# Own products of four token tiles in one stretch, another order of the first steps, short warming products and shifted due times

## The chip, the cores and the metric

The kernel runs on one core of one Trainium2 chip. The metric is device microseconds of one execution: the median of several runs. A trace is taken of one execution. TensorE (PE) multiplies matrices, VectorE (DVE), ScalarE (ACT) and GpSimd (POOL) work element by element, and SyncE (SP) issues the DMA transfers.

## What is computed

An attention-like scan over 4 batches, 8 heads, 768 tokens, head width 32 and state width 16, in chunks of 32 tokens, is followed by two feed-forward layers of width 256 to 2048 to 256 over all 3072 tokens. All is fp32.

```python
# attention, per chunk of 32 tokens
CB = np.einsum('bhin,bhjn->bhij', Cc, Bc)
M = CB * L                                   # L: decays within the chunk, causal
y_intra = np.einsum('bhij,bhjd->bhid', M, xc)
y_inter = np.einsum('bhin,bhnd->bhid', Cc, state) * decay_to_i[:, :, :, None]
y[:, :, sl] = y_intra + y_inter
state = decay_full[:, :, None, None] * state + np.sum(Bx, axis=2)
...
h = x @ w_in                                 # layer 1
x = np.maximum(0.01 * h, h) @ w_out
...
h = x @ w_in2                                # layer 2
out = (h * np.cos(h)) @ w_out2
```

## The kernel before

**Tiling.** The 3072 tokens are six blocks of 512; a block is 128 tokens of each batch, so four token tiles of 128 tokens (one for each batch). Attention runs in chunks of 64 tokens. Every fp32 product of the feed-forward layers is made of three fp32r products: the operands are split into a high part (hi) and a remainder (lo), and hi·hi, lo·hi and hi·lo are added in PSUM. ScalarE makes most of the hi parts, GpSimd and VectorE make lo.

**Stages.** `attention(b)` (L802) makes the layer's input x1h/x1l for block b. For block 0 each tile goes by itself: `cb` (L661, products of C and B), `products` (L709: y within the chunk and the new state, the "own" products), `carried` (L722, from the state before), in pairs of tiles. For blocks 1 to 5 one call does all four tiles' C·B products, two calls do the own products of two tiles each (L858 to L861, with a pause of `APART` = 4.2 planned between them, in which other products go), and one does the carried products of all four. Tile 0 and 1 of a pair hand states (st) on, which VectorE and ScalarE make from PE's results. `layer(b)` (L879) does layer 1 of blocks 0 to 3 in 16 steps f over the 2048 hidden columns: six products into h (L906 to L908), the leaky relu, the split, and six into y (L931 to L933). In blocks 0 and 1 the first `HALVES` = 3 steps are done for the first half of the tokens, then for the second half (256 columns each, L886 to L888). Blocks 4 and 5 of layer 1 and all of layer 2 go in pairs of blocks by a scheme with fewer products (`pair`, L1013; its output products are L1114 to L1116). Weights come in fp32 and are split on the chip (`weights`, L443).

**What sets the order.** Each operation is entered in a list (`Order.add`) with a due time, or with none; `set_due` (L113) then computes one backwards from what needs it, less a slack. `Order.run` (L121) plays through the program with a planned cost for each operation and lets every engine take the ready operation with the earliest due time; operations marked "turn" (the layers' products) go in a fixed order. The instructions are then issued in that order, so each engine's queue is fixed when the kernel is built. Buffers are rings of a few slots (`SLOTS`).

**Warming products.** `warm` (L315) issues products of two-byte zeros that nobody reads, so that PE has work in the head: the first `WARM_FIRST` = 11 are due before everything else, the rest fill PE's pauses in the plan until the first layer product is placed; what is left of the `WARM` = 150 is dropped. 24 of them, of 512 columns, are in the program.

Of the kernel before, what the change touches and what calls it, by code (L numbers as in the profile page):

```python
# [3 lines left out]

# [20 lines left out]
NB, H, S, D, N = 4, 8, 768, 32, 16  # L25
# [3 lines left out]
NBLK = S // T  # L29
NT = NB * NBLK  # L30
KF = DFF // 128
WARM = 150
WARM_N = 512
WARM_FIRST = 11
STEP = 2.85
PAIR_STEP = 10.6
OUT_BY = 2.0
# [6 lines left out]
ALONE = 2  # L44
SOON = 14.0
AHEAD = 8.0
WITHIN = 1.5
HEAD = 14.0
HALVES = 3
HALVED = 2  # L50
HALF_STEP = 1.55
STAGGER = 1.0
# [4 lines left out]
APART = 4.2  # L57
# [30 lines left out]
class Order:  # L88
# [24 lines left out]
    def set_due(self, after):  # L113
        for o in reversed(self.ops):
            by = o["by"] if o["by"] is not None else o["due"] if o["due"] is not None else float("inf")
            took = min(o["engines"].values()) + self.GAP + o["lag"]
            o["by"] = min([by] + [self.ops[m]["by"] - took for m in after[o["n"]]])
            if o["due"] is None:
                o["due"] = o["by"] - o["slack"]

    def run(self):  # L121
        ops, writer, readers, users = self.ops, {}, {}, {}
# [122 lines left out]
def scan_moe_kernel(ctx: ExitStack, tc, tokp, headp, abc, w_in, w_out, w_in2, w_out2, out):  # L245
# [4 lines left out]
    V, A, G, PE, SP = E["V"], E["A"], E["G"], E["P"], E["S"]  # L250
# [18 lines left out]
    od = Order(SLOTS, ("tok", "head", "abc"))  # L269
    tiles = {"A": ps.tile([128, 2, 512], F32, tag="att", bufs=1, name="att")}  # L270
# [44 lines left out]
    def warm(e, i):  # L315
        if i == 0:
            make("spread", "y", [128, H, Q], F32)
            make("warm", "h", [128, 512], F32)
        PE.matmul(tiles["warm"][:, 0:WARM_N], lhsT=tiles["zero"][:, 0:128], rhs=tiles["zero"][:, 0:WARM_N], start=True, stop=True)

    if WARM:
        od.add(-200, {"V": 0.2}, warm_zero, writes=["zero"], make=[("zero", "hi")])
        for i in range(WARM):
            od.add(-200 if i < WARM_FIRST else 1e6, {"P": WARM_N / 1200}, lambda e, i=i: warm(e, i), reads=["zero"] + (["warm/x"] if i else []),
                   writes=["warm/x"] + ([] if i else ["spread"]), make=[] if i else [("spread", "y"), ("warm", "h")], lag=-Order.GAP, spare=True)


# [474 lines left out]
    def attention(b, due, by, slack):  # L802
# [8 lines left out]
        if plain:  # L811
            od.add(due, {"N": 0.0}, fresh, reads=[f"x1h{b - 1}/fresh"] if b else [],
                   writes=[f"x1{p}{b}/fresh" for p in "hl"], make=[(f"x1{p}{b}", f"x1{p}") for p in "hl"])
# [8 lines left out]
        def on_pe(cost, group, steps, reads, writes, make=()):  # L822

            def go(e):
                for f in steps:
                    f()
            od.add(None, {"P": cost}, go, reads=reads, writes=writes, make=make, slack=min(x.slack for x in group))

        if first:
            for x in tt:  # L830
                attention_loads(x.t, x.slack)
            for i in (0, 2):
                pair = tt[i:i + 2]
                for x in pair:
                    x.prepare()
                    new = [(n, "g") for n in att_names(x.t)] if x.j == 1 else []
                    on_pe(0.6, [x], [x.cb], [*(f"x1l{b}/{j}" for j in range(i)), x.head + "/b", x.head + "/c", *(keys([x], "/y") if i else [])],
                          [*keys([x], "/cb"), *(n + "/y" for n, _ in new)], new)
                for x in pair:
                    x.decays()  # L840
                for x in pair:
                    on_pe(0.66, [x], [x.products], [x.tok + "/b", x.tok + "/x", x.ab, *keys(pair, "/cb")], [*keys([x], "/s"), *keys(pair, "/y")])
                for x in pair:
                    x.carries()
                for x in pair:
                    on_pe(0.3, [x], [x.carried], [x.head + "/c", *x.st[x.s0:2], *keys(pair, "/y")], keys(pair, "/y"))
                pair[0].outputs()
        else:
            k = Block(b, tt)
            for x in tt:  # L850
                attention_loads(x.t, x.slack)
            for x in tt:
                x.prepare()
            on_pe(1.25, tt, [k.fresh, *(lambda x=x: x.all_cb(x.j == 0) for x in tt)], [*(x.head + n for x in tt for n in ("/b", "/c")), f"run{b - 1 if b < PLAIN else b - 2}"],
                  k.keys("/cb", "/y", "/s"), [(n, "g") for n in k.names[1:]])
            for x in tt:
                x.decays()
            for i in (0, 2):  # L858
                on_pe(1.35, tt[i:i + 2], [x.products for x in tt[i:i + 2]],
                      [n for x in tt[i:i + 2] for n in (x.tok + "/b", x.tok + "/x", x.ab)] + ([f"apart{b}.0"] if i else []), k.keys("/cb", "/y", "/s"))  # L860
                od.add(None, {"D": APART}, lambda e: None, reads=k.keys("/s"), writes=[f"apart{b}.{i}"], slack=tt[0].slack)  # L861
            for s in range(1 if b == NBLK - 1 else 2):
                od.add(None, {"V": 0.36 + 0.1 * s}, lambda e, s=s: k.mask(s), reads=["own", *k.keys("/s")], writes=[tt[s].tok + "/x"], slack=tt[0].slack)
            for x in tt:
                x.carries()
            on_pe(1.2, tt, [x.all_carried for x in tt], [f"apart{b}.2", *(n for x in tt for n in (x.head + "/c", *x.st[0:2]))], k.keys("/y"))
            for s in range(2) if not plain else ():
                od.add(None, {"A": 0.6 + 0.1 * s}, lambda e, s=s: k.x_full(e, s),
                       reads=[*([n + "/y" for n in k.names[1:]] if s else ["A/y"]), *(f"x1f{b}/{c}" for c in range(2))], writes=[f"x1f{b}/{c}" for c in range(2)], slack=tt[0].slack)
            for p, e in (("h", "A"), ("l", "V")) if plain else ():  # L870
                for s in range(2):
                    od.add(None, {e: 0.6 + 0.1 * s}, lambda e, s=s, f=(k.x_hi if p == "h" else k.x_lo): f(s),
                           reads=[f"x1h{b}/fresh", f"x1l{b}/fresh", *([n + "/y" for n in k.names[1:]] if s else ["A/y"]), *([f"x1h{b}/{j}" for j in range(NB)] if p == "l" else [])],
                           writes=[f"x1{p}{b}/{j}" for j in range(NB)], slack=tt[0].slack)
# [4 lines left out]
    def layer(b, T0):  # L879

        n = NB * T
        d = STEP
# [1 line left out]
        ys = [f"y0.{b}.{c}" for c in range(2)]  # L884
        half = slice(0, n // 2), slice(n // 2, n)
        if b < HALVED:  # L886
            steps = [(f, q, T0 + (HALVES * i + f) * HALF_STEP) for i, q in enumerate(half) for f in range(HALVES)]
            T0 += 2 * HALVES * HALF_STEP - HALVES * d  # L888
        else:
            steps = []  # L890
        steps += [(f, slice(0, n), T0 + f * d) for f in range(len(steps) // 2, KF)]

        for f, q, at in steps:
            m = q.stop - q.start
# [286 lines left out]

    at = [HEAD]
    for b in range(PLAIN):
        at.append(at[b] + KF * STEP + (2 * HALVES * HALF_STEP - HALVES * STEP if b == 0 else 0))
    T0 = [at[PLAIN] - EARLY + 8 * PAIR_STEP * i for i in range(NBLK // 2 + 1)]

    weights(0, 0.0)
# [79 lines left out]
```

## Time and profile before

| | |
|---|---|
| median of 3 runs | 560.75 us (560.06 to 560.77) |
| profiled execution | 560.45 us |
| its span | 558.7 us, mean granted clock 0.99 |
| PE busy | 549.6 us, 98% of the span |
| VectorE, ScalarE, GpSimd busy | 436.5, 405.8, 251.1 us |
| HBM traffic | 46.50 MB read, 14.78 MB written, 110 GB/s over the span |

The span is cut by PE: the other engines have room on average. What PE waits for, and at which clock it runs, is in the table of waits and the table of windows. "Issue" as a releaser means that no semaphore explains the idle time. Granted clock 1.00 is 2.4 GHz, 0.50 is 1.2 GHz. A product of fp32 operands is shown in the trace as two passes, so 8 of them are x16. Times of an instruction reach from its start to its end; products overlap in PE, and the distance from start to start is what one costs in a dense row.

### The profile page before, as it was taken

How to read it: one execution, taken by the hardware profiler on the slowest of the kernel's cores; microseconds unless marked ns; L12 is line 12 of the kernel's file. 1: busy time of each engine (PE TensorE's matmuls, PEld its weight loads, DVE VectorE, ACT ScalarE, POOL GpSimd, SP SyncE). 2: the span in 40 equal slices, each digit the busy share in tenths (PEclk: the TensorE clock that was granted, in tenths of full speed). 3: DMA queues.
4: the chain of work that ended last, by engine and by line, in shares of the span. 5: the costliest groups of instructions: out<-in, count | busy, mean ns of one | idle time of the engine just before them, and what ended most of it. 6: DMA issues, size and time to landing. Idle time of an engine off the chain costs nothing.

```text
span 558.7 us, 11394 instructions
## 1 busy us (share of the span) xinstructions
PE 549.6 (98%) x4228; PEld 448.3 (80%) x4230; DVE 436.5 (78%) x833; ACT 405.8 (73%) x728; POOL 251.1 (45%) x255
## 2 busy tenths in 40 slices
PE   8899999999999999999999999999999999999996
PEld 3688897887888888888888788888888888888885
DVE  6789969998999556665655787877887878878776
ACT  4899868567668866666544788876887868867764
POOL 4502131031210644998100359955469853554540
PEclk9699999999999999999999999999999999999999
DMA  8993382757859730254344100000200000200002
GB/s 264 293 301 124 115 282 94 237 199 243 302 190 320 249 120 35 66 163 146 120 156 142 38 1 1 1 1 2 75 0 2 0 2 0 76 1 2 0 1 76
DMA packets 34632, 62.01 MB, mean 111 GB/s; under 512 B 3121, under 2 KB 12337, under 8 KB 34577
## 3 DMA queue, kind: packets, MB, share of 16 engines
q1 hardware_dynamic: 34432, 61.16, 32.9%
q8 instruction: 33, 0.54, 0.4%
q14 instruction: 23, 0.18, 0.1%
q10 hardware_dynamic: 144, 0.13, 0.1%
HBM read 46.50 MB, written 14.78 MB: 110 GB/s over the span
## 4 chain that ended last, share of the span: by engine, by line
PE 95%; DVE 2%; issue 1%; DMA 1%; ACT 0%; SPq 0%; DVEq 0%; ACTq 0%
PE h L906 6%; PE y L931 6%; PE h L907 5%; PE h L908 5%; PE y L932 5%; PE y L933 5%; PE y L1116 5%; PE h L1047 5%; PE att L1116 5%; PE y L1114 5%; PE y L1115 5%; PE att L1115 5%; PE att L1114 5%; PE h L1049 5%; PE h L1048 5%; PE g L1049 4%
## 5 line engine op out<-in xcount | busy, mean ns | idle before, releaser
L82 POOL TENSOR_TENSOR lo<-u,hi 128x512 fp32r<-128x512 f32 (+1 forms) x114 | 143.6, 1280 | 164.9 <-ACT hi L82 123.2
L82 ACT ACTIVATE hi<-u 128x512 fp32r<-128x512 f32 (+1 forms) x147 | 88.2, 614 | 10.3 <-DVE u L82 9.3
L82 ACT ACTIVATE k<-k,half_pi 128x512 f32<-128x512 f32 x96 | 68.2, 722 | 8.6 <-DVE k L82 8.4
L82 ACT ACTIVATE u<-h 128x512 f32<-128x512 f32 (+1 forms) x70 | 39.8, 570 | 40.9 <-PE h L908 40.7
L906 PE MATMUL h<-x1h,wi 128*128 128x512 f32 (+1 forms) x140 | 54.5, 389 | 0.0
L931 PE MATMUL y<-hi,wo 128*128 128x512 f32 (+1 forms) x140 | 53.4, 381 | 0.0
L907 PE MATMUL h<-x1l,wi 128*128 128x512 f32 (+1 forms) x140 | 53.0, 378 | 0.0
L908 PE MATMUL h<-x1h,wi 128*128 128x512 f32 (+1 forms) x140 | 52.9, 378 | 0.0
L932 PE MATMUL y<-hi,wo 128*128 128x512 f32 (+1 forms) x140 | 52.4, 374 | 0.0
L933 PE MATMUL y<-lo,wo 128*128 128x512 f32 (+1 forms) x140 | 52.3, 373 | 0.0
L82 DVE TENSOR_TENSOR g<-tmp,g 128x512 f32<-128x512 f32 x64 | 44.3, 692 | 8.2 <-PE g L1049 6.3
L1116 PE MATMUL y<-lo,wo 128*128 128x512 f32 x128 | 50.0, 391 | 0.3 <-DVE lo L82 0.3
L1116 PE MATMUL att<-lo,wo 128*128 128x512 f32 x128 | 49.8, 389 | 0.0
L1115 PE MATMUL y<-hi,wo 128*128 128x512 f32 x128 | 49.8, 389 | 0.0
L1115 PE MATMUL att<-hi,wo 128*128 128x512 f32 x128 | 49.8, 389 | 0.0
L1114 PE MATMUL y<-hi,wo 128*128 128x512 f32 x128 | 49.8, 389 | 0.0
L1114 PE MATMUL att<-hi,wo 128*128 128x512 f32 x128 | 49.8, 389 | 0.0
L82 ACT ACTIVATE k<-h 128x512 int32<-128x512 f32 x48 | 28.7, 597 | 23.4 <-PE h L1049 23.0
L82 DVE TENSOR_TENSOR u<-g,k 128x512 f32<-128x512 f32 x48 | 33.0, 687 | 11.5 <-ACT k L82 11.0
L82 DVE SCALAR_TENSOR_TENSOR k<-k,h 128x512 f32<-128x512 int32 x48 | 32.7, 682 | 10.0 <-ACT k L82 10.0
L82 DVE TENSOR_TENSOR lo<-u,hi 128x512 fp32r<-128x512 f32 (+1 forms) x52 | 35.5, 685 | 5.0 <-ACT hi L82 4.6
L82 ACT ACTIVATE k<-g 128x512 int32<-128x512 f32 x48 | 28.5, 594 | 12.3 <-DVE g L82 12.1
(269 smaller groups left out, 1467.1 us busy)
## 6 DMA issues: line engine op xcount, KB each, us to landing
head<-headp SPq DMA_DIRECT2D x24, 256.0 KB, 4.4
tok<-tokp SPq DMA_DIRECT2D x24, 256.0 KB, 4.9
abc<-a_clip SPq DMA_DIRECT2D x40, 128.0 KB, 3.7
raw<-w_out SPq DMA_DIRECT2D x8, 512.0 KB, 4.9
wi<-kept_wi SPq DMA_DIRECT2D x8, 512.0 KB, 4.8
wo<-kept_wo SPq DMA_DIRECT2D x8, 512.0 KB, 3.9
raw<-w_in SPq DMA_DIRECT2D x7, 512.0 KB, 4.8
ws<-kept_ws SPq DMA_DIRECT2D x8, 384.0 KB, 3.5
```

The lines of the kernel that those rows point to most:

```text
L82: self.seen.append(call(*args, **kwargs))
L906: PE.matmul(o, lhsT=wh, rhs=xh, start=(c == 0), stop=False)
L907: PE.matmul(o, lhsT=wh, rhs=xl, start=False, stop=False)
L908: PE.matmul(o, lhsT=wl, rhs=xh, start=False, stop=(c == 1))
L931: PE.matmul(o, lhsT=wh, rhs=gh, start=(f == q.start == 0), stop=False, **skip)
L932: PE.matmul(o, lhsT=wl, rhs=gh, start=False, stop=False, **skip)
L933: PE.matmul(o, lhsT=wh, rhs=gl, start=False, stop=(f == KF - 1), **skip)
L1047: PE.matmul(o, lhsT=wh, rhs=xh, start=start, stop=False, skip_group_check=True)
L1049: PE.matmul(o, lhsT=wl, rhs=xh, start=False, stop=True, skip_group_check=True)
L1114: PE.matmul(o, lhsT=wh, rhs=gh, start=begin, stop=False, skip_group_check=True)
L1115: PE.matmul(o, lhsT=wl, rhs=gh, start=False, stop=False, skip_group_check=True)
L1116: PE.matmul(o, lhsT=wh, rhs=gl, start=False, stop=end, skip_group_check=True)
```

## The change

Five things are changed. The own products of the four tiles of a block (blocks 1 to 5) are one call, hence one stretch in PE's queue, and the planned pause of 4.2 stands behind it. The warming products are of two lengths: the first 58 have 96 columns, the later ones 512. The first steps of block 0 go in the order 0, 2, 3 for each half, then 1 for all tokens. After the due times are computed, a table of seeds shifts some of them: each seed moves every operation, with a chance of 15%, by up to 3 either way; nine seeds for those due before 62, five for those due from 440 on. Constants become tuples for this.

```diff
@@ -1,5 +1,6 @@
 import bisect
 import heapq
+import random
 from contextlib import ExitStack
 
 import numpy as np
@@ -29,9 +30,9 @@
 NBLK = S // T
 NT = NB * NBLK
 KF = DFF // 128
-WARM = 150
-WARM_N = 512
-WARM_FIRST = 11
+WARM = 197
+WARM_N = 96, 512
+WARM_FIRST = 58
 STEP = 2.85
 PAIR_STEP = 10.6
 OUT_BY = 2.0
@@ -44,9 +45,11 @@
 ALONE = 2
 SOON = 14.0
 AHEAD = 8.0
+NUDGES = (-1e9, 62, (150001, 150008, 150018, 150077, 150097, 150155, 150163, 150245, 150263)), (440, 1e9, (150001, 150004, 150025, 150027, 150093))
 WITHIN = 1.5
 HEAD = 14.0
-HALVES = 3
+HALVES = 3, 3
+FIRST = (0, 2, 3, 1), (0, 1, 2)
 HALVED = 2
 HALF_STEP = 1.55
 STAGGER = 1.0
@@ -117,6 +120,13 @@
             o["by"] = min([by] + [self.ops[m]["by"] - took for m in after[o["n"]]])
             if o["due"] is None:
                 o["due"] = o["by"] - o["slack"]
+        for low, high, seeds in NUDGES:
+            some = [o for o in self.ops if not (o["spare"] or o["turn"] or set(o["engines"]) == {"N"}) and low <= o["due"] < high]
+            for seed in seeds:
+                draw = random.Random(seed)
+                for o in some:
+                    if draw.random() < 0.15:
+                        o["due"] += draw.uniform(-3, 3)
 
     def run(self):
         ops, writer, readers, users = self.ops, {}, {}, {}
@@ -316,12 +326,13 @@
         if i == 0:
             make("spread", "y", [128, H, Q], F32)
             make("warm", "h", [128, 512], F32)
-        PE.matmul(tiles["warm"][:, 0:WARM_N], lhsT=tiles["zero"][:, 0:128], rhs=tiles["zero"][:, 0:WARM_N], start=True, stop=True)
+        w = WARM_N[i >= WARM_FIRST]
+        PE.matmul(tiles["warm"][:, 0:w], lhsT=tiles["zero"][:, 0:128], rhs=tiles["zero"][:, 0:w], start=True, stop=True)
 
     if WARM:
         od.add(-200, {"V": 0.2}, warm_zero, writes=["zero"], make=[("zero", "hi")])
         for i in range(WARM):
-            od.add(-200 if i < WARM_FIRST else 1e6, {"P": WARM_N / 1200}, lambda e, i=i: warm(e, i), reads=["zero"] + (["warm/x"] if i else []),
+            od.add(-200 if i < WARM_FIRST else 1e6, {"P": WARM_N[i >= WARM_FIRST] / 1200}, lambda e, i=i: warm(e, i), reads=["zero"] + (["warm/x"] if i else []),
                    writes=["warm/x"] + ([] if i else ["spread"]), make=[] if i else [("spread", "y"), ("warm", "h")], lag=-Order.GAP, spare=True)
 
 
@@ -855,10 +866,8 @@
                   k.keys("/cb", "/y", "/s"), [(n, "g") for n in k.names[1:]])
             for x in tt:
                 x.decays()
-            for i in (0, 2):
-                on_pe(1.35, tt[i:i + 2], [x.products for x in tt[i:i + 2]],
-                      [n for x in tt[i:i + 2] for n in (x.tok + "/b", x.tok + "/x", x.ab)] + ([f"apart{b}.0"] if i else []), k.keys("/cb", "/y", "/s"))
-                od.add(None, {"D": APART}, lambda e: None, reads=k.keys("/s"), writes=[f"apart{b}.{i}"], slack=tt[0].slack)
+            on_pe(2.5, tt, [x.products for x in tt], [n for x in tt for n in (x.tok + "/b", x.tok + "/x", x.ab)], k.keys("/cb", "/y", "/s"))
+            od.add(None, {"D": APART}, lambda e: None, reads=k.keys("/s"), writes=[f"apart{b}.2"], slack=tt[0].slack)
             for s in range(1 if b == NBLK - 1 else 2):
                 od.add(None, {"V": 0.36 + 0.1 * s}, lambda e, s=s: k.mask(s), reads=["own", *k.keys("/s")], writes=[tt[s].tok + "/x"], slack=tt[0].slack)
             for x in tt:
@@ -884,11 +893,13 @@
         ys = [f"y0.{b}.{c}" for c in range(2)]
         half = slice(0, n // 2), slice(n // 2, n)
         if b < HALVED:
-            steps = [(f, q, T0 + (HALVES * i + f) * HALF_STEP) for i, q in enumerate(half) for f in range(HALVES)]
-            T0 += 2 * HALVES * HALF_STEP - HALVES * d
+            m = HALVES[b]
+            steps = [(f, q, T0 + (m * i + j) * HALF_STEP) for i, q in enumerate(half) for j, f in enumerate(FIRST[b][:m])]
+            T0 += 2 * m * HALF_STEP - m * d
         else:
-            steps = []
-        steps += [(f, slice(0, n), T0 + f * d) for f in range(len(steps) // 2, KF)]
+            m, steps = 0, []
+        fs = [*FIRST[b], *range(len(FIRST[b]), KF)] if b < HALVED else range(KF)
+        steps += [(f, slice(0, n), T0 + j * d) for j, f in enumerate(fs) if j >= m]
 
         for f, q, at in steps:
             m = q.stop - q.start
@@ -1181,7 +1192,7 @@
 
     at = [HEAD]
     for b in range(PLAIN):
-        at.append(at[b] + KF * STEP + (2 * HALVES * HALF_STEP - HALVES * STEP if b == 0 else 0))
+        at.append(at[b] + KF * STEP + (2 * HALVES[0] * HALF_STEP - HALVES[0] * STEP if b == 0 else 0))
     T0 = [at[PLAIN] - EARLY + 8 * PAIR_STEP * i for i in range(NBLK // 2 + 1)]
 
     weights(0, 0.0)
```

The effect on the order is shown at three places. Line numbers after the change are higher by 3 in the helper (L85 for L82) and by 11 in the attention and layer code.

First PE in the head, where the attention of tiles 0 and 1 ends and the first layer product (L906, later L917) follows; L729 and L740 are the carried products of tile 1 (st is its state), L319 and L330 the warming products, L671 and L682 the C·B products of tiles 2 and 3, L647 and L658 spread decays. Before:

```order
L647 MATMUL y<-lo,u 128x512 x2
L729 MATMUL att<-head,st_281 32x64 x4
L729 MATMUL g<-head,st_281 32x64 x4
L319 LDWEIGHTS hi
L319 MATMUL h<-hi 128x512
...
L671 MATMUL att<-head 64x128 x8
L671 MATMUL g<-head 64x128 x8
L906 MATMUL h<-x1h,wi 128x256
```

After:

```order
L740 MATMUL att<-head,st_328 32x64 x4
L740 MATMUL g<-head,st_328 32x64 x4
L658 MATMUL y<-lo,u 128x512 x2
L330 LDWEIGHTS hi
L330 MATMUL h<-hi 128x512
...
L682 MATMUL att<-head 64x128 x8
L917 MATMUL h<-x1h,wi 128x256
...
L682 MATMUL g<-head 64x128 x8
```

The carried products of tile 1 now stand ahead of a pair of spread products, five warming products of 512 columns follow (six before), and tile 3's C·B products (g) have moved behind the first six layer products. Ahead of all this the 13 first warming products have become 58 short ones and 5 long ones, so that 49 more pairs of load and product stand before the same real work.

Next VectorE at the same time: st_281, later st_328, is tile 1's state, abc<-y,ident the scan of the decays of tile 2, head and tok its factors. Before:

```order
L82 SCALAR_TENSOR_TENSOR st_226<-st_217,tok,att 128x64
L82 TENSOR_TENSOR abc<-g,abc 128x256 x2
L82 SCALAR_TENSOR_TENSOR abc<-y,ident 128x512
L82 SCALAR_TENSOR_TENSOR tok<-starts,tok 128x64
L82 TENSOR_TENSOR tok<-tok,abc 128x128
L82 TENSOR_TENSOR head<-head,tok 128x2x64
```

After:

```order
L85 SCALAR_TENSOR_TENSOR st_278<-st_269,tok,att 128x64
L85 TENSOR_TENSOR abc<-g,abc 128x256 x2
L85 SCALAR_TENSOR_TENSOR abc<-y,ident 128x512
L85 COPY st_328<-g 128x64
L85 TENSOR_TENSOR tok<-tok,abc 128x128
L85 SCALAR_TENSOR_TENSOR st_334<-st_328,tok,g 128x64
```

The copy that makes tile 1's state is VectorE's now and stands behind the scan; two operations on head and tok have gone to GpSimd.

Last PE in block 3's attention, at the seam of the two stretches of own products (L715 and L719, later L726 and L730). Before:

```order
L719 MATMUL att<-tok 32x64 x4
L719 MATMUL g<-tok 32x64 x4
L931 MATMUL y<-hi,wo 128x512
...
L908 MATMUL h<-x1h,wi 128x512
L715 MATMUL att<-abc,tok 32x64 x4
```

After:

```order
L730 MATMUL att<-tok 32x64 x4
L730 MATMUL g<-tok 32x64 x4
L726 MATMUL att<-abc,tok 32x64 x4
L726 MATMUL g<-abc,tok 32x64 x4
...
L917 MATMUL h<-x1h,wi 128x512
```

The 21 layer products between the second and the third tile's own products are gone from there; the layer's products follow the fourth tile's.

## Rows read from the trace of the kernel before

**Rows 1.** The page: span, busy time of the engines, the instruction queue.
```profile
span 558.7 us, 11394 instructions
...
PE 549.6 (98%) x4228; PEld 448.3 (80%) x4230; DVE 436.5 (78%) x833; ACT 405.8 (73%) x728; POOL 251.1 (45%) x255
...
q8 instruction: 33, 0.54, 0.4%
```
**Rows 2.** Waits of PE: us in total, times, longest us.
```profile
PE g L671 <- issue: 1.0, 1, 1.0
...
PE att L729 <- DVE st L82: 0.4, 1, 0.4
PE att L715 <- ACT st L82: 0.3, 1, 0.3
```
**Rows 3.** Windows: us, busy time (x) by engine, granted clock, DMA share, GB/s.
```profile
18.06:28.30 10.24, 9.47 (x159) 8.27 (x158) 6.82 (x16) 8.43 (x20) 5.99 (x8) 0.50 0.90 281
28.30:548.50 520.20, 520.20 (x3826) 428.74 (x3826) 411.83 (x777) 385.04 (x686) 236.85 (x225) 1.00 0.31 102
```
**Rows 4.** Timeline of PE in the head: start, us, instruction, count, idle before.
```profile
1.25 3.17 PE L319 MATMUL h<-hi 128*128 128x512 bf16 x7 [1.25 <-DVE hi L82]
...
8.61 0.67 PE L671 MATMUL g<-head 64*64 64x128 f32 x16 [0.61 <-DMA head<-headp]
...
10.19 0.73 PE L647 MATMUL y<-lo,u 8*128 8x512 f32 x2 [0.25 <-DVE tok L82]
...
13.51 1.24 PE L319 MATMUL h<-hi 128*128 128x512 bf16 x5 [0.16 <-issue]
...
15.69 0.61 PE L671 MATMUL g<-head 64*64 64x128 f32 x15
17.27 0.32 PE L671 MATMUL g<-head 64*64 64x128 f32 x1 [0.97 <-issue]
17.52 0.38 PE L906 MATMUL h<-x1h,wi 128*128 128x256 f32 x1
...
21.58 0.86 PE L729 MATMUL att<-head,st 32*32 32x64 f32 x8
22.14 0.44 PE L729 MATMUL g<-head,st 32*32 32x64 f32 x8
```
**Rows 5.** DMA queues in 9.7:14.7, 14.7:15.8, 19.7:20.7, 55.6:56.7: packets, MB, share.
```profile
q1 hardware_dynamic: 1181, 1.95, 105.7%
...
q8 instruction: 1, 0.02, 5.9%
...
q8 instruction: 1, 0.02, 5.6%
...
q8 instruction: 1, 0.02, 5.8%
```
**Rows 6.** Timeline of PE around a two-tile stretch of block 1.
```profile
53.95 0.39 PE L933 MATMUL y<-lo,wo 128*128 128x512 f32 x1
54.27 0.26 PE L715 MATMUL att<-abc,tok 64*32 64x64 f32 x4
...
55.24 0.27 PE L719 MATMUL g<-tok 64*32 64x64 f32 x4
...
55.77 0.39 PE L932 MATMUL y<-hi,wo 128*128 128x512 f32 x1
```
**Rows 7.** Timeline of VectorE in the head.
```profile
11.08 1.21 DVE L82 TENSOR_TENSOR_SCAN abc<-y,ident 128x512 f32<-128x512 f32 x1
...
15.07 0.48 DVE L82 TENSOR_TENSOR x1l<-g,x1h 128x128 fp32r<-128x128 f32 x2
```
**Rows 8.** Timeline of VectorE and PE in the tail.
```profile
548.45 1.89 DVE L82 TENSOR_TENSOR lo<-u,hi 128x512 fp32r<-128x512 f32 x3
...
548.52 0.39 PE L1115 MATMUL y<-hi,wo 128*128 128x512 f32 x1
549.19 0.50 PE L1116 MATMUL y<-lo,wo 128*128 128x512 f32 x1 [0.28 <-DVE lo L82]
```

## The prediction

> **What bounds the kernel now.** I read the page first: TensorE (PE) is busy 549.6 of 558.7 us [rows 1]. The list of PE's waits comes next, because it tells where the other 9 us are: the long ones lie in the head or the tail, and the largest that no semaphore explains, 1.0 us of "issue" ahead of L671, stands in the head [rows 2]. Then the table of windows: from 28.30 to 548.50 PE is busy 520.20 of 520.20 us at a granted clock of 1.00; from 18.06 to 28.30 it is granted 0.50, that is 1.2 GHz instead of 2.4 GHz [rows 3]. The reader should take from this that the real products are a fixed load, and the diff changes none of them. Time can move in four places only: the head up to about 30 us, the borders of the attention stretches, stops of PE that no other engine causes, and the tail. The profiled execution took 560.45 us, its span 558.72 and 1.73 around it; it lies 0.3 us under the median of 560.75. The sum below is made against 560.45 and 0.3 is added at the end.
>
> **PE's instruction refills.** The page has a queue of the kind "instruction": 33 transfers, 0.54 MB, so 16 KB each [rows 1]. PE's 4228 products and 4230 loads over 33 are 256 instructions a transfer. I counted PE's instructions from the head of its list: a product of two-byte numbers or of fp32r is 2 with its weight load, an fp32 product 4, a wait that stands alone 1. The "issue" stop, from the end of 15 of L671's 16 passes (15.69 and 0.61 long) to the 16th at 17.27 [rows 4], falls on instruction 450. A second, shorter stop lies in L729 (8 passes take 0.86 from 21.58, [rows 4]); by the count it holds instruction 706, exactly 256 later. One refill transfer lies in 14.7 to 15.8 and one in 19.7 to 20.7 [rows 5]; each time PE goes on some 1.5 us after the transfer (17.27 after 15.8; 22.14 after 20.7, [rows 4, 5]). So I read both stops as PE waiting for its own code: instructions 450 to 705 are asked for when 194 is executed (near 9.7 us), and queue behind the data loads then under way (from 9.7 to 14.7 the data queue moves 1.95 MB and no code moves at all, [rows 5]). Where DMA is quiet, boundary 1218 is executed at 54.5 and its transfer lies in 55.6 to 56.7 [rows 5]: 1.1 to the start, 1.0 for itself, 1.5 until PE may use it, 3.6 us together. 256 instructions that pass faster than this delay stop PE. Dense 512-column products need 128 × 0.23 = 29 us for 256; 64-column attention products do not.
>
> The Trainium skill (Runtime: NRT & Kernel Launch, section Instruction fetch mechanics) has the same 16 KiB blocks of 256 instructions for PE, but calls the crossing of a boundary "mostly hidden". The trace agrees on the block and disagrees in the head, where about 1 us is not hidden. By that rule no stop would be added here; this is the first rival.
>
> **Head: +3.0 us.** The order puts 58 warming products of 96 columns and 15 of 512 in place of 24 of 512: 49 pairs, 98 instructions more before the same real work. Boundary 450 therefore comes 98 instructions earlier in it, no longer in the second product of L671 on tile 2 but inside the carried products of tile 1 (L740 on st_328). On VectorE the scan of tile 2's decays (1.21 us, [rows 7]) now stands ahead of the copy that makes st_328, so PE wants these products at about 14.0 instead of 13.0. Boundary 194 lies right behind tile 1's L671 now, which cannot start before its data are there at 8.61 and takes 0.5 [rows 4]: it is executed at 9.1 instead of 9.7. The code comes sooner by no more than these 0.6: 17.27 − 0.6 = 16.7. That is a stop of 2.7 us in place of 1.0. Behind it stand, in this order: the rest of the carried products 0.3, two spread products 0.73 [rows 4], five warming products, and the attention product L682. The stop leaves PE idle, and before the clock fell to 0.50 right behind the stop of 1.0 us; so I take the five at half clock: 7 took 3.17 at 1.2 GHz and 5 took 1.24 at 2.4 GHz [rows 4], so 5 take 2.1 (1.2 if the clock holds). L682 takes 0.6. The sum is 16.7 + 0.3 + 0.7 + 2.1 + 0.6 = 20.4 for the first layer product, against 17.52 [rows 4]: +2.9. VectorE's last step between them and L682, x1l, takes 0.48 [rows 7] and fits beside the warming products, so it adds nothing. The second L682 moves behind this product, where it costs 0.9 at half clock: +0.9. Steps 2 and 3, now ahead of step 1, give PE 12 products among the attention of tiles 2 and 3, where before the waits for st, 0.4 and 0.3 [rows 2], and the second refill's 0.3 stood (0.86 for 8 passes, against 0.44 for the next 8, [rows 4]): −1.0. Boundary 706 now has the long way from 16.9 to about 26, so its refill is hidden. From 0 to 1.2 may come on top where the first output products wait for split weights or for lo, which PE reaches after 18 products without the earlier pauses; I take 0.2, near the low end, since before there is no wait in the table from 28.30 on [rows 3]. +2.9 + 0.9 − 1.0 + 0.2 = +3.0. The ends: +0.5 if the stop is short (1.0 as before) and the clock holds, +4.5 with all waits and clock losses. The clock's return at 28.3 is taken as unchanged.
>
> **Merged stretches: −1.7 us.** In block 1 a stretch of two tiles lies between the product at 53.95 and the second big one at 55.77, 1.82 us; less two product spacings (0.23) this is 1.37, and its 96 pairs of load and product take 1.02 from 54.27 to the last group (55.24 and a part) [rows 6]. So 0.35 is paid for entering and leaving. Five blocks have one such entry less: −1.7. It is nothing only if the seam is paid inside the stretch; at most −1.9.
>
> **Refills in merged stretches: +2.3 us.** A merged stretch is 384 instructions in a row, 192 pairs, 2.05 us at the rate above. It can hold two boundaries, which two stretches of 192, with dense products between, never did. By the count the five stretches start at 1278, 2303, 3199, 4027 and 4905. The boundaries at 194 + 256k fall 196 in (block 1), 195 in (block 2), 67 and 323 in (block 3), 7 and 263 in (block 4), and 153 in (block 5). Where there is one, its code had 29 us or more to come. In block 3 the second is wanted 128 pairs = 1.36 us after the first was executed, and the delay is 3.6: a stop of 2.2. I take 2.0, since the window around the transfer is a little wider than the transfer. In block 4 the first boundary is only 7 in. If PE's sequencer asks for code as it reads ahead of the slow products, it asks before the stretch begins, by an unknown time: 0 to 2.2 as in block 3. I take 0.3, nearer to the refills behind 28.30, none of which stops PE [rows 3]. Nothing covers such a stop: the whole machine follows PE. 2.0 + 0.3 = 2.3; the ends are 0 and 4.4.
>
> **Tail: −0.4 us.** PE stands still ahead of L1116 at 549.19, for DVE's three lo in a row from 548.45 [rows 8]: from the product at 548.52 to it are 0.67, less a spacing of 0.23 is 0.44. The new order puts the first of these lo two operations earlier, between a k and a u. The wait goes; next in line are lo two and three, which in the new order stand behind one u each and are wanted later. 0 to −0.6, taken −0.4.
>
> The other edits (tuples for constants, another label for the block's last stretch) issue the same products, and the two decay operations that move to GpSimd in the head lie beside PE's stop: 0.
>
> **Sum:** +3.0 − 1.7 + 2.3 − 0.4 = +3.2, so 563.65 for the profile and 563.9 beside the median.
>
> **The rivals.**
> *Refills stay hidden (faster).* The stops belong to something else at those two places, or code that is due earlier is also asked for earlier. For it: 31 of 33 refills stop nothing. Against it: two stops exactly 256 instructions apart, each about 1.5 us after a code transfer. Then the head has no stop: carried products to 14.4, spread 15.1, five warming products at full clock 16.3, L682 16.8, so −0.7, +0.5 for the second L682 at full clock, −1.0 for the waits, +0.2: −1.0. With −1.7 − 0.4 the sum is −3.1: 557.6. If the clock then does not fall at all, half of the 10.24 us goes too, about 552.5. It decides as soon as PE shows no "issue" stop over 1 us before the first layer product. Chance 0.2.
> *Head as forecast, but no stop in the middle:* code is kept far enough ahead once DMA is quiet (before, no refill behind 28.30 stops PE, [rows 3]). +3.0 − 1.7 − 0.4 = +0.9: 561.6. Chance 0.17.
> *Worse:* full stop in blocks 3 and 4 (4.4), head +4.5 since the clock comes back later and output products wait, seams −1.4, tail 0: +7.5, 568. For it: the head's order was set for due times, not for code arrival, and block 4's boundaries are 256 apart like block 3's. Chance 0.13.
> *The change doesn't do what it says:* the short products do not raise the clock by 4.4 us, so cb and the spreads of the first tiles run slower, 1 to 2 us. They lie before the stop, which hides them; this changes no case.
>
> **How the numbers follow.** The forecast has 0.5, with its own range of 561.8 to 566.0. A measurement of this kernel tells 0.2%, 1.1 us, from no change, so same is 559.6 to 561.9. Faster: 0.2 from the first rival, and 0.06 from low ends of the others. Same: 0.12 of the second rival's 0.17 and 0.03 of the forecast. Slower is the rest, 0.59. The range 557.2 to 567.0 leaves about 0.1 on either side: a clock that stays up, and the full worse case.
>
> **What would show it.** In the profile after: an "issue" stop of 2 to 3 us of PE in L740 near 14 to 17 us; the first layer product (L917) at 20 to 21; another "issue" stop of about 2 us in the stretch of block 3 (L726/L730), five sixths through it; none, or a short one, in block 4; one big product late per stretch instead of two; no wait of the tail's L1127 for lo. The prediction is wrong if the code stops are missing, or if the clock's stretch at 0.50 is shorter than 8 or longer than 13 us.

## The result and the profile after

The changed kernel takes 563.21 us in the median of 6 runs, 560.40 before: 1.0055 times before, 95% interval 1.0034 to 1.0076, so some 3.1 us slower. The forecast was 563.9, slower. The profiled execution took 563.31 us. Its single runs go from 560.1 to 564.4, those before from 559.0 to 561.5. The granted clock goes with them: the mean over the run is 0.997 in the fastest of the six and 0.989 in the slowest.

The page after, span, busy time and instruction queue ([rows 1] before):

```profile
span 561.6 us, 11476 instructions
...
PE 550.9 (98%) x4279; PEld 451.4 (80%) x4279; DVE 436.4 (78%) x837; ACT 407.4 (73%) x728; POOL 244.1 (43%) x251
...
q8 instruction: 33, 0.54, 0.4%
```

The whole list of PE's waits after (us in total, times, longest), against [rows 2]:

```profile
PE att L726 <- issue: 2.4, 1, 2.4
PE h L330 <- DVE hi L85: 1.3, 1, 1.3
PE att L740 <- issue: 1.1, 1, 1.1
PE y L943 <- DVE wo L85: 0.8, 1, 0.8
PE att L740 <- DVE st L85: 0.4, 2, 0.3
PE att L730 <- issue: 0.4, 1, 0.4
```

Three stops are "issue", which no semaphore explains: in L740 in the head, in L726 and in L730. These are the places that the count of instructions gave: the carried products of tile 1, and the merged stretches of blocks 3 and 4. The wait of the tail's products for lo is gone. A wait for a split weight (wo, 0.8) is new.

The head in PE's timeline after ([rows 4] before):

```profile
13.26 0.31 PE L740 MATMUL att<-head,st 32*32 32x64 f32 x6 [0.29 <-DVE st L85]
14.62 0.24 PE L740 MATMUL att<-head,st 32*32 32x64 f32 x1 [1.05 <-issue]
...
15.54 2.16 PE L330 MATMUL h<-hi 128*128 128x512 bf16 x5
17.63 1.13 PE L682 MATMUL att<-head 64*64 64x128 f32 x16
18.69 0.58 PE L917 MATMUL h<-x1h,wi 128*128 128x256 f32 x1
...
25.58 0.39 PE L943 MATMUL y<-hi,wo 128*128 128x256 f32 x1 [0.82 <-DVE wo L85]
```

PE stops six passes into tile 1's carried products, as forecast, but for 1.05 us instead of 2.7. The five warming products take 2.16, the price of half clock. The first layer product starts at 18.69, not at 20.4. The trace has the first code transfer from 12.12 to 13.10, where before it began at 14.7 [rows 5]; PE goes on 1.5 us behind its end, as before. The granted clock of the head, from the table of windows after (columns as in [rows 3]):

```profile
16.30:17.30 1.00, 1.00 (x4) 0.22 (x2) 1.00 (x2) 1.00 (x2) 1.00 (x3) 0.50 0.92 258
...
19.30:25.80 6.50, 5.51 (x163) 4.26 (x163) 4.94 (x14) 5.18 (x13) 1.75 (x4) 1.00 0.63 210
...
26.20:29.00 2.80, 2.80 (x15) 2.80 (x15) 2.79 (x7) 2.48 (x5) 0.47 (x1) 0.50 0.77 228
```

Before, one stretch of 10.24 us was at 0.50; after, there are two of 3.4 us, the first behind the code stop, the second behind the wait for wo.

Block 3 in PE's timeline after, where before two stretches ran without a stop:

```profile
130.45 0.39 PE L919 MATMUL h<-x1h,wi 128*128 128x512 f32 x1
135.01 0.26 PE L726 MATMUL att<-abc,tok 64*32 64x64 f32 x4 [2.41 <-issue]
...
135.52 0.79 PE L917 MATMUL h<-x1h,wi 128*128 128x512 f32 x1
136.11 0.63 PE L918 MATMUL h<-x1l,wi 128*128 128x512 f32 x1
...
138.65 0.39 PE L943 MATMUL y<-hi,wo 128*128 128x512 f32 x1
138.88 0.40 PE L944 MATMUL y<-lo,wo 128*128 128x512 f32 x1
```

The stop of 2.41 is followed by seven big products at 1.2 GHz: from 135.52 to 138.65 they take 3.13 us, where seven spacings of 0.23 are 1.6. The window there has the granted clock at 0.50 (columns as in [rows 3]):

```profile
136.00:137.00 1.00, 1.00 (x4) 0.71 (x4) 1.00 (x6) 0.00 (x0) 0.00 (x0) 0.50 0.79 209
```

So the stop costs 2.4 and some 1.5 more. Block 4 has a short stop without this:

```profile
162.90 0.25 PE L730 MATMUL att<-tok 64*32 64x64 f32 x3 [0.44 <-issue]
163.71 0.50 PE L917 MATMUL h<-x1h,wi 128*128 128x512 f32 x1
164.05 0.40 PE L918 MATMUL h<-x1l,wi 128*128 128x512 f32 x1
```

To see where the time went, I compared when PE has started the same amount of real products (each weighted with its cost at full clock, 526.8 us in all, warming left out). After minus before, in the two profiled executions:

| real products done | before at | after at | lag |
|---|---|---|---|
| 30 (behind the head) | 49.62 | 50.13 | +0.5 |
| 90 (behind blocks 1 and 2) | 112.87 | 112.50 | −0.4 |
| 120 (behind block 3) | 144.13 | 147.47 | +3.3 |
| 140 (behind block 4) | 164.71 | 168.42 | +3.7 |
| 200 (behind block 5) | 226.77 | 230.01 | +3.2 |
| 520 | 546.93 | 550.49 | +3.6 |
| last product | 554.10 | 557.06 | +3.0 |

Head +0.5, blocks 1 and 2 −0.9, block 3 +3.7, block 4 +0.4, block 5 −0.5, tail −0.6, and 0.3 on the long way between. These are differences of two single executions, and the 10.24 us at 1.2 GHz of the one before are much for its program: two runs below with the head of the kernel before (the merge alone, and the old head with blocks 3 and 5 merged) had 3.4 us of it. Counted in the same way they are, behind the head, 1.1 and 0.8 us ahead of the kernel before.

### The profile page after: what moved, and what is told of

It is laid out like the page before. It is cut to its first block, busy times and chain, and to the rows that moved or that the text cites. A ratio compares the mean times of both kernels' runs of the same rounds, so it can differ in the third digit from the quotient of the medians.

```text
span 561.6 us, 11476 instructions
## 1 busy us (share of the span) xinstructions
PE 550.9 (98%) x4279; PEld 451.4 (80%) x4279; DVE 436.4 (78%) x837; ACT 407.4 (73%) x728; POOL 244.1 (43%) x251
## 4 chain that ended last, share of the span: by engine, by line
PE 96%; DVE 1%; issue 1%; DMA 1%; SPq 0%; POOL 0%; ACT 0%; POOLq 0%; DVEq 0%
PE h L917 6%; PE y L942 6%; PE y L943 5%; PE y L944 5%; PE h L918 5%; PE h L919 5%; PE y L1127 5%; PE y L1125 5%; PE y L1126 5%; PE att L1127 5%; PE att L1126 5%; PE att L1125 5%; PE h L1058 5%; PE h L1060 5%; PE h L1059 5%; PE g L1060 4%
## 5 line engine op out<-in xcount | busy, mean ns | idle before, releaser
L85 POOL TENSOR_TENSOR lo<-u,hi 128x512 fp32r<-128x512 f32 (+1 forms) x111 | 141.4, 1294 | 202.5 <-ACT hi L85 163.7
L85 ACT ACTIVATE hi<-u 128x512 fp32r<-128x512 f32 (+1 forms) x146 | 88.4, 618 | 9.3 <-DVE u L85 7.9
L85 ACT ACTIVATE k<-k,half_pi 128x512 f32<-128x512 f32 x96 | 67.8, 722 | 7.8 <-DVE k L85 7.3
L85 ACT ACTIVATE u<-h 128x512 f32<-128x512 f32 (+1 forms) x70 | 40.0, 571 | 40.4 <-PE h L919 40.1
L917 PE MATMUL h<-x1h,wi 128*128 128x512 f32 (+1 forms) x140 | 54.1, 386 | 0.0
L85 DVE TENSOR_TENSOR g<-tmp,g 128x512 f32<-128x512 f32 x64 | 44.3, 692 | 8.9 <-PE g L1060 6.9
L85 ACT ACTIVATE k<-h 128x512 int32<-128x512 f32 x48 | 28.7, 597 | 23.8 <-PE h L1060 23.3
L85 DVE TENSOR_TENSOR lo<-u,hi 128x512 fp32r<-128x512 f32 (+1 forms) x55 | 35.9, 654 | 6.3 <-ACT hi L85 6.2
L85 DVE SCALAR_TENSOR_TENSOR k<-k,h 128x512 f32<-128x512 int32 x48 | 32.6, 682 | 9.8 <-ACT k L85 9.7
L85 DVE TENSOR_TENSOR u<-g,k 128x512 f32<-128x512 f32 x48 | 33.0, 687 | 8.5 <-ACT k L85 8.0
L85 ACT ACTIVATE k<-g 128x512 int32<-128x512 f32 x48 | 28.5, 594 | 12.3 <-DVE g L85 12.1
```

Source lines behind the costliest of these rows:

```text
L85: self.seen.append(call(*args, **kwargs))
L917: PE.matmul(o, lhsT=wh, rhs=xh, start=(c == 0), stop=False)
```

## The experiments

The theory on trial (code theory): PE stops where it passes two boundaries of its 256-instruction code blocks in less time than a refill takes. The rivals: the stop belongs to block 3's data or waits; or the loss is that of the shifted due times. Comparisons are with runs of the kernel before on the same chip; its median there was 559.1 to 559.7. Each program ran 4 to 12 times. A place in a stretch is the number of PE's instructions from its start to the boundary.

**Fewer instructions, same warming time.**

```diff
-WARM = 197
-WARM_N = 96, 512
-WARM_FIRST = 58
+WARM = 166
+WARM_N = 206, 512
+WARM_FIRST = 27
...
-{"P": WARM_N[i >= WARM_FIRST] / 1200}
+{"P": 4.64 / 27 if i < WARM_FIRST else 512 / 1200}
```

> The changed kernel with 27 first warming products of 206 columns in place of 58 of 96: the same columns and the same planned time, 62 instructions fewer on PE ahead of everything else. Code theory (PE stops where a merged stretch holds two boundaries of its 256-instruction code blocks and the second comes too soon): by the count the boundaries now fall 2 and 258 into the stretch of block 1, 1 and 257 in block 2, 129 in block 3, 69 and 325 in block 4, 215 in block 5. Block 3 loses its stop of 2.4 us; block 4 gets one of 2.2 to 2.6 with the same stretch of half clock behind it, in place of 0.44; blocks 1 and 2 get none or up to 0.5 each. Time within 1.5 us of the changed kernel's 563.2. Rival (the stop belongs to block 3 itself: its data, its waits): the 2.4 us stay in block 3, block 4 keeps 0.44, and no stop moves.

566.08 us, 1.0102 (1.0072 to 1.0132). PE's waits that are "issue":

```profile
PE h L917 <- issue: 3.0, 1, 3.0
PE att L726 <- issue: 2.1, 1, 2.1
PE g L726 <- issue: 1.5, 1, 1.5
...
PE g L730 <- issue: 0.4, 1, 0.4
```

In PE's timeline:

```profile
137.63 0.79 PE L917 MATMUL h<-x1h,wi 128*128 128x512 f32 x1 [3.05 <-issue]
...
167.09 0.26 PE L726 MATMUL att<-abc,tok 64*32 64x64 f32 x4 [2.09 <-issue]
```

The stop in block 4 came, so the place hangs on the number of instructions ahead, and block 3's data are out. Two things were a miss. Block 3 did not get free: with the first boundary 129 in, the second falls on the first product behind the stretch (385 of 384), and PE stops there for 3.0 (L917 at 137.63). I had drawn the line at 128; it must be later, because the first products behind a stretch do not yet give the refill time enough. And block 1, with a boundary 2 in, stopped for 1.5, while block 2, with one 1 in, did not stop. Their code transfers began at different times: in block 1 0.4 us behind the boundary (56.99), in block 2 3.0 us ahead of it (95.63 for 98.66). The time was 2.9 above the changed kernel's median, 1.4 more than the expected bound. The "issue" of 0.4 at L730 is in the head.

**The merge alone.**

```diff
-            for i in (0, 2):
-                on_pe(1.35, tt[i:i + 2], [x.products for x in tt[i:i + 2]],
...
+            on_pe(2.5, tt, [x.products for x in tt], [n for x in tt for n in (x.tok + "/b", x.tok + "/x", x.ab)], k.keys("/cb", "/y", "/s"))
```

(made in the kernel before, without the change's other edits)

> The kernel before with only the own products of the four tiles merged (blocks 1 to 5). Code theory: boundaries fall 39 and 295 into block 1's stretch, 45 and 301 in block 2, 166 in block 3, 110 and 366 in block 4, 226 in block 5. Stops of about 2.4 us in blocks 1, 2 and 4, none in 3 and 5; with 1.6 of half clock behind each and a seam of 0.35 saved in all five: 3 x 4.0 - 1.7 = about +10 us against before, 567 to 572. Rival (the stop belongs to block 3): one stop in block 3, about +2.3, 562 to 564. Second rival (merging costs nothing, the stop came from the shifted due times): five seams saved, 558.7.

569.86 us, 1.0167 (1.0131 to 1.0203): 9.4 us slower by the ratio, 10.0 at the last product of the profiled execution. The three stops in PE's timeline:

```profile
59.43 0.31 PE L715 MATMUL att<-abc,tok 64*32 64x64 f32 x4 [1.75 <-issue]
60.29 0.79 PE L904 MATMUL h<-x1h,wi 128*128 128x512 f32 x1
...
102.54 0.24 PE L715 MATMUL att<-abc,tok 64*32 64x64 f32 x2 [1.60 <-issue]
...
167.93 0.24 PE L719 MATMUL att<-tok 64*32 64x64 f32 x1 [3.43 <-issue]
```

They stand in blocks 1, 2 and 4 and not in 3 and 5, as counted. Both rivals fail here. Big products at 1.2 GHz follow each of the three, 3.4 us of them.

**Block 3 in two stretches again.**

```diff
+            if b in (3,):
+                for i in (0, 2):
+                    on_pe(1.35, tt[i:i + 2], [x.products for x in tt[i:i + 2]], ...
+            else:
                 on_pe(2.5, tt, [x.products for x in tt], ...
```

> The changed kernel with block 3's own products in two stretches again, as before; the others stay merged. Code theory: boundaries then fall 98 into the first and 119 into the second stretch of block 3, with dense products between, so the stop of 2.4 and the half clock behind it (together about 4 us) go and a seam of 0.35 comes back: 559.0 to 560.5, which is 1 us under the kernel before. Block 4 keeps its small stop (6 and 262 in). Rival (the loss is that of the new due times, spread over the blocks): gain under 1.5 us, 562 or more.

559.08 us, 0.9983 (0.9964 to 1.0003): 4.1 under the changed kernel's median, as expected; from the kernel before it can't be told apart. "Issue" waits left (the edit moves lines by 6; L948 is the output product):

```profile
PE att L740 <- issue: 2.2, 1, 2.2
...
PE y L948 <- issue: 0.8, 1, 0.8
```

Its profiled execution is its slowest run, 561.42. The head's program is that of the changed kernel, yet the code stop in L740 is 2.2 here and 1.1 there: the code transfer lies at 13.60 to 14.71 instead of 12.12 to 13.10. So the head's stop varies from run to run; how much of the spread of the times is due to it was not measured. The 0.8 is block 5, where the boundary is 142 in. Block 4's small stop, expected to stay, is not there: with the boundary 6 in (7 in the changed kernel), its transfer began 3.2 us ahead of it (155.54), there 0.4 ahead.

**The same with eight instructions more** (62 first warming products of 90 columns).

```diff
-WARM_N = 96, 512
-WARM_FIRST = 58
+WARM_N = 90, 512
+WARM_FIRST = 62
```

> As the run with block 3 split, and with 62 first warming products of 90 columns in place of 58 of 96, which puts 8 instructions more ahead of everything: no merged stretch holds two boundaries (188, 187, 254 and 134 in). Code theory: block 4's stop of 0.44 goes too, 0.3 to 0.5 us under that run. Rival: no difference between the two.

560.32 us, 1.0002 (0.9986 to 1.0018), so not faster than the run before it: a miss. Block 4 has no stop, but it had none there either, and block 5, now 134 in, has one of 1.1 on the first products behind the stretch:

```profile
PE h L925 <- issue: 1.1, 1, 1.1
PE y L949 <- DVE wo L85: 0.8, 1, 0.8
PE att L740 <- issue: 0.7, 1, 0.7
```

134, 142 and 153 instructions in thus gave 1.1, 0.8 and none. Each product more behind the stretch gives the refill 0.23 us, but the refill itself varies: from the boundary to PE's next product it took 3.2 us here (190.94 to 194.19) and 3.8 with 142 (192.30 to 196.13), so that four products, 0.9 us, made a difference of 0.3. The 1.2 us between the medians of the two runs is not explained by this; their intervals overlap.

**No merge at all, head and tail changed** (the edit of block 3, for blocks 1 to 5: `if b in (1, 2, 3, 4, 5)`).

> The changed kernel with the own products of every block in two stretches again, so that only the head (short warming products, order of the first steps, shifted due times) and the tail differ from the kernel before. This weighs the head term by itself. By the profile of the changed kernel the head costs about +0.5 us (0 to +2, since the length of its code stop hangs on how many loads are queued when the code is asked for) and the tail gives 0.6: 559 to 561, no difference from before. By the forecast's head term (+3.0) it would be 562.0 to 562.6. Code theory: no stop over 0.3 us between 34 and 540 us.

560.77 us, 1.0017 (1.0003 to 1.0031), or +0.9 us (0.2 to 1.7). No "issue" wait is listed between 34 and 556 us. If the tail gives 0.6, as in the profiled execution, the head costs +1.5 (0.8 to 2.3): half of the forecast's +3.0. It is more than the +0.5 of the two profiled executions, which fits the 10.24 us at 1.2 GHz of the one before: against the two runs with the same head, 1.1 and 0.8 ahead of it, the +0.5 is +1.3 to +1.6.

**Only merges without a second boundary near by, 62 products** (`if b in (3, 5)` split).

> As the run with block 3 split and 62 first warming products, and with block 5's own products in two stretches as well, since there the second boundary came just behind the merged stretch. Blocks 1, 2 and 4 stay merged with boundaries 188, 187 and 254 in. Code theory: no stop over 0.3 us behind the head; three seams saved (about 0.44 each by the changed kernel's blocks 1 and 2), the tail's 0.6, head 0 to +1: 1.5 us under the kernel before, 557.5 to 559.2. If stops come at other places, 560 or more.

559.03 us, 0.9987 (0.9972 to 1.0002). No code stop behind the head, as expected. The gain in the mean is 0.7 (between 1.6 and −0.1), where 1.5 was expected; a head that costs 1.5 instead of 0 to 1 would account for it.

**The same with 72 products of 77 columns.**

> The same with 72 first warming products of 77 columns: 20 instructions more ahead of everything. Boundaries 168, 167 and 234 into the merged stretches, so still no stop there. In the head the first refill is asked for sooner, but its code is wanted 20 instructions sooner in the real work, by about 0.5 us: the same time as the run with 62 within 0.7 us.

559.25 us, 0.9996 (0.9980 to 1.0011): 0.2 us from the run with 62 by the medians, 0.5 by the ratios, so within the 0.7 expected; no "issue" wait over 0.2 us is listed.

**The short warming products alone** (58 of 96 columns, then 512, in the kernel before).

```diff
-WARM = 150
-WARM_N = 512
-WARM_FIRST = 11
+WARM = 197
+WARM_N = 96, 512
+WARM_FIRST = 58
```

> The kernel before with only the short warming products (58 of 96, then 512), so with some 94 instructions more ahead of the same work; stretches, steps and due times as before. Code theory: the head's first code stop moves from the C-B products of tile 2 to the products or carried products of tile 1, and is 1 to 2.5 us long; behind the head nothing changes, as a stretch of two tiles never holds two boundaries. 559 to 562 us. By the forecast's way of counting (+2.9 for the first layer product) 562 or more.

560.29 us, 1.0017 (1.0005 to 1.0029), +0.95 us. The head's first code stop moved to tile 1's products, as counted:

```profile
PE att L730 <- issue: 1.4, 1, 1.4
```

So the short warming products may well be the larger part of what the head costs: 0.95 of 1.5. The intervals (0.3 to 1.6, and 0.8 to 2.3) are too wide to say more, and this run's profiled execution, 0.7 us under that of the kernel before, doesn't show the loss.

**The old head, blocks 3 and 5 merged** (first warming products, `FIRST` = (0, 1, 2) and the head's seeds as before the change; `if b in (1, 2, 4)` split).

> The head of the kernel before (11 first warming products of 512, steps 0, 1, 2, no shifted due times in the head), the tail's shifted due times, and merged own products in blocks 3 and 5 alone, where by the count the boundaries fall 205 and 249 into the merged stretch. Code theory: no stop behind the head; two seams saved (0.44 each), tail 0.6, head as before: 1.5 us under the kernel before, 557.5 to 558.5. If the head of the changed kernel cost nothing, this is no better than the run with blocks 1, 2 and 4 merged (0.6 under before): 558.5 to 559.2.

558.85 us, 0.9987 (0.9973 to 1.0002). No code stop of 0.4 or more anywhere. The time lies in the second expectation, that of a head that costs nothing, but its interval (557.8 to 559.4) reaches far into the first and doesn't tell them apart. The first code stop of the head, 1.0 in the profiled execution before, is 0.3 here with the same head.

**The old head with 36 of 156 columns, blocks 1, 2 and 5 merged** (`WARM_N = 156, 512`, `WARM_FIRST = 36`, `if b in (3, 4)` split).

> The same, but with 36 first warming products of 156 columns (50 instructions more ahead of everything), and blocks 1, 2 and 5 merged instead: boundaries 245, 251 and 155 in. Code theory: no stop behind the head, three seams saved, tail 0.6: 1.9 us under before if the head is as before; its first code stop lies 50 instructions earlier in the same work, in the warming products ahead of tile 2's C-B products or in these, and may add 0 to 1.5 us: 557 to 559.3.

558.98 us, 0.9986 (0.9970 to 1.0002). The time is in the expected range, but "no stop behind the head" was a miss. Its profiled execution, the slowest of its runs (561.02), has one in block 1:

```profile
PE g L726 <- issue: 2.0, 1, 2.0
PE att L726 <- DVE abc L85: 1.4, 2, 0.8
```

The stretch begins 11 instructions behind one boundary, so the next comes 245 in. PE stood at a wait for abc just ahead of the stretch, and the transfer began 2.8 us after the boundary (52.6 to 55.4). A boundary just ahead of the stretch can thus count like one in it. It need not: in five other merged stretches with a boundary 2 to 7 ahead (block 2 here and in the next run, block 4 in the two runs with 62 warming products, block 5 in the run before this one) the transfer began 2.8 to 3.4 us before the boundary ran, and none has a stop. So at the edge of a stretch the start of the transfer, and not the count alone, tells the stops from the rest.

**The same without block 1's merge, blocks 2, 3 and 5 merged** (`if b in (1, 4)` split).

> The run with 36 first warming products of 156 columns and the old head's order, with the own products of blocks 1 and 4 in two stretches and those of 2, 3 and 5 merged. The run before it still had a stop of 2.0 us and a stretch of half clock in block 1, whose merged stretch began 11 instructions behind a boundary while the refill came late (2.8 us from boundary to transfer). Code theory: without that merge the 3.9 us that its trace lost there are gone; boundaries 252, 154 and 171 into the merged stretches, no stop behind the head: 555.5 to 557.5, at least 2 us under the kernel before. If its median of 558.98 did not hang on block 1's stop: 558.5 to 559.5.

558.07 us, 0.9980 (0.9969 to 0.9990): 1.1 us under the kernel before, and the only version that beats both kernels clear of noise. Its waits of PE, the whole list:

```profile
PE h L330 <- DVE hi L85: 1.3, 1, 1.3
PE att L726 <- DVE abc L85: 0.9, 1, 0.9
PE att L726 <- ACT st L85: 0.6, 1, 0.6
PE att L740 <- DVE st L85: 0.6, 1, 0.6
PE att L682 <- DVE x1l L85: 0.5, 1, 0.5
```

Not one stop is "issue". The time missed the expected range by 0.6 and fell by 0.9 from the run with block 1 merged, not by 2. By the ratios it is 0.3, so the two runs can't be told apart: the stop in block 1 was read from that run's slowest execution, and whether most of the others had it is not known.

## Why the prediction was right, and which of its terms were not

- **What bounds the kernel: right.** PE has the same load; the lag arises in the head, in blocks 3 and 4, and is given back at seams and tail.
- **Refills as the cause: right, and shown.** Programs with four different counts have their stops where the count puts them (blocks 3 and 4; 4, 1 and behind 3; 1, 2 and 4; behind 5). The count alone is not enough where a boundary lies at the start of a stretch: there PE stopped 0.44, 1.5 or not at all, as the transfer began 0.4 us ahead of the boundary, 0.4 behind it, or 3 ahead. The forecast left this open for block 4. The first rival, refills hidden, is out, and so is the second, no stop in the middle. The sentence of the Trainium skill (Runtime: NRT & Kernel Launch, section Instruction fetch mechanics) that a crossing is "mostly hidden" holds for most of the 33 crossings; the trace differs from it in the head, and in block 3, where two crossings would come 1.5 us apart without the stop (131.10 and 132.60) and PE stops for 2.41.
- **Head +3.0: mechanism right, size wrong.** It measured +0.5 in the profiled execution and +1.5 (0.8 to 2.3) in the mean, if the tail gives 0.6. Of the forecast's signs, a stop of 2 to 3 us and the first layer product at 20 to 21 did not come (1.05 and 18.69). The step that failed is "The code comes sooner by no more than these 0.6". It came 2.65 sooner (14.62 against 17.27). The forecast moved the request by 0.6 and left the queue of loads ahead of it as it was; from boundary to transfer it was 5.0 before, and 3.5 here, 4.5 and 4.1 in the two runs with block 3 split. After the change SP issues one 512 KB load (of w_out) at 9.08 us, behind boundary 194 at 8.60; before, it was issued at 9.31, ahead of that boundary at 9.70. At the 390 GB/s of that stretch it is 1.3 us. In the run with block 3 split the load went out at 8.83, ahead of the boundary at 9.13, and the stop was 2.2. That this race makes the spread was not tested by moving the load alone, and the run with 72 products speaks against it as the whole cause: there the load went out at 8.16, ahead of the boundary at about 8.4, and the code transfer began at 10.24 already. Why the transfer began sooner stays open.
- **Clock: wrong.** "The clock's return at 28.3 is taken as unchanged": it fell twice, for 3.4 us each, which is under the 8 us that the forecast named as a sign against it. The moved L682 (19.79, 0.67 long) therefore cost no half clock. Before, too, the stretch is not fixed: the programs with the same head had 3.4 us of it. In the 35 executions of the kernel before that four of the experiments are compared with, the profiled execution's mean clock of 0.99 comes once; 13 runs at 0.992 to 0.994 took 560.2 us in the median, 17 at 0.995 to 0.997 took 559.0.
- **Merges −1.7: a little low.** Blocks 1 and 2 gave 0.44 each, which is −2.2 for five.
- **Refills in stretches +2.3: right in place, short by half in price.** Block 3: the stop is 2.41 against 2.0, but the forecast had no term for what follows it, the 1.5 us of seven products at 1.2 GHz. Block 4: 0.44 against 0.3. Single boundaries had less time than the forecast's "29 us or more": in block 1 5.7 us from one to the next (52.16 to 57.85). That was still enough.
- **Tail −0.4:** −0.6.

So the total was met by luck: the head was set 1.5 too high and block 3 some 1.9 too low. The direction hung on neither: with the head alone put right the sum is +1.7, with block 3 alone +5.1.

## What to carry to other kernels

A queue of short products has a code budget: count PE's instructions, find the boundaries every 256, and do not let two of them fall within the time of one refill: 3.0 to 5.5 us from the boundary to PE's next product in the stops here, except where the transfer began ahead of the boundary. An edit that saves seams by joining short stretches, or that only changes how many warming products stand in front, moves all these boundaries; merging all five blocks cost 9.4 us in one program, while a program with three blocks merged at chosen offsets, other warming products and the shifted tail is 1.1 us faster than the kernel before. An "issue" stop that no semaphore explains should be priced with the slow products behind it, if the clock falls, and not with its own length alone. And one profiled execution need not be typical: look at the granted clock of the other runs before a difference of 1 us is read from two profiles.

## What the runs showed of the hardware that was not expected

- From the end of a code transfer to PE's next product it is nearly constant in the head: 1.52 (13.10 to 14.62), 1.44 (14.71 to 16.15), 1.47 (12.73 to 14.20), 1.49 before (15.78 to 17.27). In block 3 after it is 1.23 (133.78 to 135.01).
- The refill's start is not: 0.9 us behind the boundary in block 3 after (131.10 to 131.98), 2.8 in block 1 of the run with 36 products, 3.5 to 5.0 in the head of the kernels before and after and of the two runs with block 3 split, where data loads are under way (the DMA share is 1.04 from 9 to 12.1 us in the changed kernel), and 1.8 in the head of the run with 72 products.
- PE's sequencer reads ahead of slow products: in block 4 after, the transfer for boundary 4034 began at 160.55, before the product at that boundary ran (160.96). There the stop was 0.44 with the boundary 7 in; in block 1 with 27 warming products, 2 in, the transfer began 0.4 us behind the boundary and the stop was 1.5; in the run with block 3 split, 6 in, the transfer began 3.2 us ahead of it and there was no stop. What sets how far ahead PE reads was not tested.
